# Two DMAs and a VectorE addition in place of a folding product between two MLP layers, with a new order of issue

## The chip, the cores and the metric

One core of one Trainium2 chip. The metric is the device time of one execution in microseconds (us); lower is better. A change within 0.2% cannot be told from none here.

## What is computed

Tokens are 2 x 4096 rows of 192 floats. A causal window of 7 rows is mixed with softmax weights per head, then two MLP layers follow, both 192 to 2048 to 192, in fp32:

```python
w = exp(weight_gen - max); w = w / (sum(w) + 1e-09)
x = einsum('bshk,bskhg->bshg', w, windows_of_7(x_pad))      # 8 heads, 24 columns each
h = x @ moe_w_in;   x = (h * sigmoid(h)) @ moe_w_out         # layer 1
h = x @ moe2_w_in                                            # layer 2
P = a[0] + a[1]*h + a[2]*h**2 + a[3]*h**3
Q = 1.0 + abs(b[0])*abs(h) + abs(b[1])*h**2
out = (P / (Q + 1e-06)) @ moe2_w_out
```

## The kernel before, in words

The 8192 tokens are worked in 16 blocks of 512, with the tokens along the free axis. The 192 columns are held as 128 rows and 64 more, the 64 stored twice in one 128-row half (`DL` is 64). Every operand of a product is split into a rounded high part and a low rest. The hidden 2048 rows are cut into 8 units of 256, so that a unit's intermediate is one PSUM tile of 128x1024 (the tag `h`, two buffers). The letters below are the names in the plan; a digit behind a letter is the unit.

- Attention of a block: loads `X` and `AW`, four rows of work `M`, `p`, `r`, `a` (VectorE or GpSimd, L436 to L455), a DMA `AD` that doubles the 64 columns, transposes `T` on TensorE, then `XH0` (ScalarE) and `XL0` (VectorE) split the result.
- Layer 1, unit u: product `A` (10 matmuls, L516), SiLU `S` in place (ScalarE, L553), its rounded part `H` (ScalarE, L557), the rest `L` (VectorE, L561), product `C` into the accumulator `acc0` (10 matmuls).
- Between the layers: the second half of `acc0` holds partial sums of the 64 columns on rows 0 to 63 and on rows 64 to 127. `EC` copies this half to SBUF, `EM` multiplies it with the matrix `fold` (two identities side by side, so that both row halves receive the sum) back into `acc0`; `XH1` and `XL1` split the result for layer 2.
- Layer 2, unit u: product `B`, then four readers of its PSUM tile: `U` (L592) and `V` (L596) on ScalarE, `u` (L602) and `w` (L605) on VectorE. The denominator goes `Y` (VectorE, L611), `N` (logarithm, ScalarE, L616), `G` (sigmoid, ScalarE, L619); `g` (VectorE, L622) makes the ratio, `h` and `l` split it, product `D` adds to `acc1`.
- The end of a block: `FC` copies `acc1` to the SBUF tile `of`, `FT` turns it back on TensorE, `FE` moves the result to the SBUF tile `o`, `O` stores it by DMA.
- Weights arrive as 64-bit floats and are decoded at the start, four VectorE operations for each piece, interleaved with blocks 0 and 1.

Nothing is scheduled at run time. A table of numbers (`KEYS`) gives each step a key; block b of the middle blocks adds 72 times b. All steps are sorted by key and issued in that order, each engine executing its own in order. A second table (`ENGINES`) picks one of the engines that a step may use. Blocks of a layer overlap: while block b is in layer 2, block b+1 is in layer 1 and the last units of layer 2 of block b-1 finish. Buffers are counted in `BUFS`; a step that takes a buffer waits for the last reader of its former content. Readers of one PSUM tile on different engines wait for one another in the order of issue. All DMAs leave from one queue, SyncE's.

Of the kernel before, what the change touches and what calls it, by code (L numbers as in the profile page):

```python
# [19 lines left out]
JB = 4  # L20
# [23 lines left out]
    q0B03:-316.92 q0A12:-309.71 q0B04:-303.11 s0n:-287.19 q0A2a:-276.83 q0B0d:-276.41 q0O11:-275.19 q0B0h:-271.54
    q0A13:-270.4 zM0:-265.19 q0O12:-257.47 q0A21:-246.3 q0A14:-238.64 zp0:-238.19 q0A22:-237.38 zr0:-229.4
    q0A23:-224.88 za0:-219.64 q0O13:-215.26 zM1:-214.13 q0A24:-200.03 q0O6l:-191.2 q0A3l:-175.29 q0A1h:-175.16
    q0A1x:-172.73 q0A3a:-168.08 zp1:-167.7 q0B1l:-164 q0A31:-160.72 q0O6a:-160.16 zr1:-157.97 q0O61:-156.06
    za1:-153.62 q0O62:-150.5 zM2:-148.24 q0O14:-147.91 zp2:-143.67 q0A32:-141.33 q0A2h:-139.04 zr2:-130.1
    q0B0x:-129.28 X:-122.84 za2:-121.15 q0O1h:-119.09 q0O63:-116.78 q0O3l:-114.33 zM3:-113.33 q0B1a:-108.33
    q0O1x:-107.5 zp3:-105.83 q0A33:-104.78 AW:-103.75 zr3:-103.7 M0:-102 q0B11:-99.99 p0:-99.17 q0O64:-98.62 r0:-95.49  # L50
    q0O3a:-95.08 za3:-94.88 q1A0l:-93.71 q0B12:-93.54 q0A34:-92.42 a0:-91.77 q0O31:-91.43 q0O6h:-90.26 M2:-89.49
    q0A2x:-89.37 q0B13:-87.76 zAD:-87.54 q0O32:-85.82 zT:-85.5 zXH0:-84.82 p2:-84.81 r2:-82.87 q0B14:-81.83 s1l:-79.62
    a2:-78.91 q0A3h:-77.37 s1m:-77.25 M1:-76.38 s1e:-75.48 zXL0:-74.15 q0O6x:-73.97 p1:-73.06 q0A3x:-72.06 r1:-70.26
    a1:-69.45 q1A0a:-68.21 q0O4l:-67.96 M3:-67.93 s1n:-67.64 q0O33:-67.46 q0O4a:-66.3 q0B1d:-63.09 q0B1h:-58.98
    p3:-58.27 q0O41:-58.11 r3:-57.41 a3:-56.23 zA0:-55.29 q1A01:-53.55 AD:-52.97 q1B0l:-52.39 q0O34:-52.26 s1s:-52.14
    q1B0a:-49.67 q0O42:-45.37 q1B1l:-41.31 q1A02:-40.81 q1B01:-38.11 zA1:-37.66 q1A03:-37.49 q1B02:-37.18 q0O3h:-36.98
    q1A04:-35.54 q0O3x:-35.3 zS1:-33.17 zS0:-32.69 T:-32.52 q1B03:-32.4 zH0:-31.67 q0O7l:-31.25 XH0:-30.06
    q1B04:-27.57 XL0:-26.97 zL0:-26.04 zA2:-25.83 q0O43:-25.64 zC0:-25.16 zH1:-25.08 A1:-23.94 q0O7a:-23.54
    q0B1x:-23.34 S1:-20.68 q1B0d:-19.55 q0O71:-19.39 zL1:-19.32 zS2:-19.15 cr:-18.63 zC1:-18.63 H1:-18.34 zA3:-18.22
    A0:-17.92 S0:-17.74 H0:-17.7 q0O44:-17.4 q0O5l:-17.27 L1:-17.17 L0:-15.84 q0O72:-14.6 zH2:-12.31 A2:-12.19  # L60
    C0:-11.95 S2:-11.05 zL2:-10.62 q0O5a:-10.18 H2:-9.74 q0O51:-9.49 q0O73:-8.85 zS3:-8.43 zH3:-8.32 L2:-7.53
    q1B0h:-6.59 q0O52:-6.44 zA4:-6.32 A3:-6.25 zL3:-4.99 zS4:-4.81 zC2:-3.95 C1:-3.35 q0O74:-3.01 q1B0x:-2.84 S3:-2.08
    q0O4h:-1.67 zA5:-0.78 q1B1a:0.17 zS5:0.67 H3:1.05 q0O53:1.19 L3:1.38 zH4:1.61 q1A3l:1.94 zC3:2.03 q0O4x:2.33
# [5 lines left out]
    L7:39.16 zL7:39.78 q1O0a:40.59 q1A1a:40.61 q1O01:41.22 q1A11:42.51 C7:42.68 zC6:44.87 q1A12:45.54 zC7:46.34
    zEC:47.04 EC:47.63 q1O02:47.96 EM:48.17 q1A13:48.18 q1B14:49.89 zEM:49.99 q1A33:50.18 q1A14:50.33 q1B1d:50.75  # L70
    XH1:50.98 q1A1h:52.25 zXH1:52.35 q1A1x:53.2 XL1:54.32 zXL1:54.44 zB2:55.99 B2:56.94 zU2:57.59 q1O03:57.63
    q1A34:58.12 q1O04:58.57 q1A3h:58.58 U2:59.61 V2:60.06 zu2:60.2 zV2:60.24 zw2:60.55 u2:60.8 q1O1l:60.82 q1A3x:60.89
    zY2:61.22 w2:61.87 zB0:62.37 B0:63.3 q1B1h:64.35 q1B1x:64.57 q1O1a:64.77 V0:65.24 q1O11:65.24 U0:65.35 Y2:66.19
# [653 lines left out]
```

## Time and profile before

| | |
|---|---|
| time, median of 3 runs | 1407.87 us (1406.32 to 1409.04) |
| time of the profiled execution | 1408.39 us |
| its span, first to last instruction | 1406.6 us |
| TensorE (PE) busy | 1247.3 us, 89% of the span, 5472 matmuls |
| VectorE (DVE) busy | 1144.8 us, 81% |
| ScalarE (ACT) busy | 1044.6 us, 74% |
| GpSimd (POOL) busy | 586.3 us, 42% |
| mean granted TensorE clock | 0.986 of full |

A busy share is the time in which an engine executes; the rest it waits, by its order, for another engine or a buffer. The rows further below come from views of one execution: the page, the table of busy time by stretch, the timeline of an engine, the chain of waits that ended last, and one line's durations.

### The profile page before, as it was taken

To read this page: it belongs to the slowest core of one execution; us is meant where nothing else is said; L and a number is where in the kernel's file an instruction comes from. 1 tells how busy PE (TensorE), PEld (TensorE's weight loads), DVE (VectorE), ACT (ScalarE), POOL (GpSimd) and SP (SyncE) were. 2 spreads that over 40 slices of the span, in tenths; PEclk is the share of its full clock that TensorE was granted. 3 is DMA by queue.
4 is the path that set the end of the run, shared out by engine and by line. 5 is a ranking of instruction groups with operands and counts; after the bars stand their busy time and mean duration, and the time that the engine had idled before them with its cause. 6 is when DMAs were issued, how large, how long until landed. Compare 5 with 4: busy or idle time off the path is not lost.

```text
span 1406.6 us, 14510 instructions
## 1 busy us (share of the span) xinstructions
PE 1247.3 (89%) x5472; PEld 1001.1 (71%) x5472; DVE 1144.8 (81%) x1073; ACT 1044.6 (74%) x1000; POOL 586.3 (42%) x328
## 2 busy tenths in 40 slices
...
DMA packets 24294, 45.00 MB, mean 32 GB/s; under 512 B 10404, under 2 KB 16674, under 8 KB 24224
## 3 DMA queue, kind: packets, MB, share of 16 engines
...
q8 instruction: 43, 0.70, 0.2%
...
## 4 chain that ended last, share of the span: by engine, by line
PE 63%; DVE 19%; issue 8%; ACT 7%; DMA 2%; SPq 0%; POOL 0%; DVEq 0%; ACTq 0%; POOLq 0%
PE h L516 33%; PE acc L540 5%; PE acc L537 5%; PE acc L538 5%; PE acc L539 5%; PE acc L541 5%; DVE t L602 5%; DVE t L605 4%; ACT y L596 3%; DVE g1l L561 2%; ACT t L592 2%; DVE y L611 1%; PE acc L577 1%; DMA aw<-wsm 1%; DVE pr L445 1%
## 5 line engine op out<-in xcount | busy, mean ns | idle before, releaser
L516 PE MATMUL h<-xh,wa 128*128 128x512 f32 x1024 | 329.6, 403 | 94.4 <-DVE g1l L561 55.3
L516 PEld LDWEIGHTS h<-xh,wa 128*128 128x128 f32 x1024 | 187.3, 191 | 159.9 <-issue 64.3
L217 POOL TENSOR_SCALAR g2h<-t 128x1024 fp32r<-128x1024 f32 x93 | 119.9, 1289 | 405.7 <-PE acc L539 388.6
L602 DVE TENSOR_TENSOR t<-t,h 128x1024 f32<-128x1024 f32 x128 | 155.4, 1215 | 101.0 <-ACT y L596 48.1
L632 POOL TENSOR_TENSOR g2l<-t,g2h 128x1024 fp32r<-128x1024 f32 x88 | 223.9, 2546 | 22.3 <-ACT g2h L215 14.5
L596 ACT ACTIVATE y<-h,b_sb 128x1024 f32<-128x1024 f32 x128 | 142.5, 1113 | 120.6 <-PE h L516 86.1
L611 DVE SCALAR_TENSOR_TENSOR y<-y,b_sb 128x1024 f32<-128x1024 f32 x128 | 205.2, 1615 | 25.0 <-ACT y L596 24.9
L592 ACT ACTIVATE t<-h,a_sb 128x1024 f32<-128x1024 f32 x128 | 153.9, 1203 | 68.6 <-PE h L516 67.6
L516 PE MATMUL h<-xl,wa 128*128 128x512 f32 x512 | 202.2, 395 | 2.3 <-DVE xl L493 2.3
L561 DVE TENSOR_TENSOR g1l<-h,g1h 128x1024 fp32r<-128x1024 f32 x128 | 156.0, 1219 | 57.4 <-ACT g1h L557 57.3
L516 PE MATMUL h<-xh,wb 128*128 128x512 f32 x512 | 202.3, 395 | 0.0
L516 PE MATMUL h<-xl,wb 128*128 128x512 f32 x512 | 201.5, 394 | 0.0
L622 DVE SCALAR_TENSOR_TENSOR t<-t,a_sb,y 128x1024 f32<-128x1024 f32 x128 | 188.1, 1489 | 2.6 <-ACT y L619 2.5
L436 POOL TENSOR_TENSOR pr<-xw,aw 128x1344 f32<-128x1344 f32 x45 | 139.2, 3093 | 117.9 <-DVE ao L455 117.9
L553 ACT ACTIVATE h<-h 128x1024 f32<-128x1024 f32 x128 | 129.0, 1008 | 62.5 <-PE h L516 59.0
L605 DVE SCALAR_TENSOR_TENSOR t<-t,a_sb,h 128x1024 f32<-128x1024 f32 x128 | 163.7, 1280 | 14.1 <-ACT y L596 9.8
L616 ACT ACTIVATE y<-y,c_sb 128x1024 f32<-128x1024 f32 x128 | 146.6, 1148 | 9.3 <-DVE y L611 8.9
L557 ACT ACTIVATE g1h<-h 128x1024 fp32r<-128x1024 f32 x128 | 130.8, 1023 | 16.7 <-PE acc L539 14.3
L619 ACT ACTIVATE y<-y 128x1024 f32<-128x1024 f32 x128 | 125.9, 1048 | 0.4
L516 PEld LDWEIGHTS h<-xl,wa 128*128 128x128 f32 x512 | 97.5, 190 | 24.7 <-DVE xl L493 3.4
L516 PEld LDWEIGHTS h<-xh,wb 128*128 128x128 f32 x512 | 97.7, 191 | 21.5
L516 PEld LDWEIGHTS h<-xl,wb 128*128 128x128 f32 x512 | 97.4, 190 | 21.3
...
## 6 DMA issues: line engine op xcount, KB each, us to landing
...
raw<-in_moe_w_out_dram SPq DMA_DIRECT2D x16, 384.0 KB, 3.2
out_dram<-o SPq DMA_DIRECT2D x16, 384.0 KB, 5.8
...
dup<-dec SPq DMA_DIRECT2D x16, 128.0 KB, 2.3
ao<-ao SPq DMA_DIRECT2D x16, 128.0 KB, 2.4
...
```

The costliest lines, as they stand in the source:

```text
L436: e.tensor_tensor(out=p.rearrange("p k (h g) -> p k h g", g=G), in0=st[xw][:, j:j + K, :].rearrange("p k (h g) -> p k h g", g=G), in1=weig ...
L516: pe.matmul(out=h[:, i], lhsT=w[:, f], rhs=xx, start=(n == 0), stop=(n == len(terms) - 1))
L557: act.activation(out=t, in_=st[hb], func=AF.Copy)
L561: dve.tensor_tensor(out=t, in0=st[hb], in1=st[gh].bitcast(F32), op=ALU.subtract)
L592: act.activation(out=q, in_=st[hb], func=AF.Identity, scale=a_sb[:, 3:4], bias=a_sb[:, 2:3])
L596: act.activation(out=q, in_=st[hb], func=AF.Abs, scale=b_sb[:, 1:2])
L602: dve.tensor_tensor(out=st[t], in0=st[t], in1=flat(), op=ALU.mult)
L605: dve.scalar_tensor_tensor(out=st[t], in0=st[t], scalar=a_sb[:, 1:2], in1=flat(), op0=ALU.add, op1=ALU.mult)
L611: dve.scalar_tensor_tensor(out=st[y], in0=st[y], scalar=b_sb[:, 0:1], in1=st[y], op0=ALU.add, op1=ALU.mult)
L616: act.activation(out=st[y], in_=st[y], func=AF.Ln, scale=c_sb[:, 0:1], bias=1e-6)
L622: dve.scalar_tensor_tensor(out=st[t], in0=st[t], scalar=a_sb[:, 0:1], in1=st[y], op0=ALU.add, op1=ALU.mult)
L632: e.tensor_tensor(out=q, in0=st[t], in1=st[gh].bitcast(F32), op=ALU.subtract)
```

## The change

The folding product `EM` goes. The tile `of` in the role of `e` now has two halves: `EC` copies into the first, two DMAs (`EM`, now on SyncE's queue) write the first's rows 64 to 127 into the second's rows 0 to 63 and the other way round, and a VectorE addition `EA` adds the second half to the accumulator in PSUM. The tile `o` is gone: `FE` writes its result over `of`, and `O` stores from there, so that the next `EC` must wait until that store has read it. The buffers of `y` go from 4 to 5. Block 1 gets keys of its own (prefix y), as blocks 0 (z) and 15 (e) had; all keys and the choice of engines are new.

```diff
-    zEC:47.04 EC:47.63 EM:48.17 q1A13:48.18 q1B14:49.89 zEM:49.99 q1A33:50.18 q1A14:50.33 q1B1d:50.75
+    yS3:47.283 q1O3x:47.615 EC:47.948 EM:48.099 yH3:48.169 zB3:48.825 zU3:49.187 yC1:51.102 q1O63:51.941 yL3:53.318
...
 BUFS = dict(
-    h=2, acc0=1, acc1=1, xw=1, aw=2, pr=1, ao=1, xh0=1, xl0=1, xh1=1, xl1=1, of=1, o=1,
-    g1h=2, g1l=2, y=4, t=5, g2h=2, g2l=2,
+    h=2, acc0=1, acc1=1, xw=1, aw=2, pr=1, ao=1, xh0=1, xl0=1, xh1=1, xl1=1, of=1,
+    g1h=2, g1l=2, y=5, t=5, g2h=2, g2l=2,
 )
...
         def copy(e):
-            st[ev] = t = new("of", [P, 2 * BT], name="e")[:, 0:BT]
-            round_to(e, t, st[acc][:, 1])
+            st[ev] = t = new("of", [P, 2 * BT], name="e")
+            round_to(e, t[:, 0:BT], st[acc][:, 1])
+
+        def swap(e):
+            t = st[ev]
+            for i in range(2):
+                sp.dma_start(out=t[i * DL:(i + 1) * DL, BT:], in_=t[(1 - i) * DL:(2 - i) * DL, 0:BT])
 
         def sums(e):
-            pe.matmul(out=st[acc][:, 1], lhsT=fold, rhs=st[ev], start=True, stop=True)
+            dve.tensor_tensor(out=st[acc][:, 1], in0=st[acc][:, 1], in1=st[ev][:, BT:], op=ALU.add)
...
-        plan.op("EM", b, "PE", sums, rd=[(*ev, 0), ("ident", 0)], wr=[(*acc, 0)])
+        plan.op("EM", b, "SP", swap, rd=[(*ev, 0)], wr=[(*ev, 0)])
+        plan.op("EA", b, "DVE", sums, rd=[(*acc, 0), (*ev, 0)], wr=[(*acc, 0)])
...
         def evac(e):
-            st[o] = t = new("o", [P, JB, D])
+            t = st[of].rearrange("p a c -> p (a c)")[:, 0:JB * D].rearrange("p (j d) -> p j d", d=D)
+            st["o", b] = t
             round_to(e, t, st[tp][:, :, 0:D])
```

All lines of the key table are replaced; the two shown are the ones with the steps between the layers. What the tables do is seen in the order in which the built programs issue.

ScalarE, a middle block, from a SiLU `S7` to the split `XH1` of the sums between the layers. Before: L553 is `S`, L557 `H`, L596 `V`, L592 `U`, L616 `N`, L619 `G`, L489 `XH`; a table load precedes a function of another kind.

```order
L553 ACTIVATE h<-h 128x1024
L616 ACT_TABLE_LOAD
L616 ACTIVATE y<-y,c_sb 128x1024
L557 ACTIVATE g1h<-h 128x1024
L596 ACTIVATE y<-h,b_sb 128x1024
L616 ACTIVATE y<-y,c_sb 128x1024
L592 ACTIVATE t<-h,a_sb 128x1024
L616 ACTIVATE y<-y,c_sb 128x1024
L489 ACTIVATE xh_4463<-tp 128x1024
L616 ACTIVATE y<-y,c_sb 128x1024
L619 ACT_TABLE_LOAD
L619 ACTIVATE y<-y 128x1024 x4
```

The same place in the changed kernel, from the logarithms `N4`, `N5` ahead of `S7`: L650 is `N`, L581 `S`, L653 `G`, L585 `H`, L243 here `FE`, L517 `XH`.

```order
L650 ACT_TABLE_LOAD
L650 ACTIVATE y<-y,c_sb 128x1024 x2
L581 ACT_TABLE_LOAD
L581 ACTIVATE h<-h 128x1024
L653 ACT_TABLE_LOAD
L653 ACTIVATE y<-y 128x1024
L585 ACTIVATE g1h<-h 128x1024
L243 ACTIVATE of<-to 128x768
L650 ACT_TABLE_LOAD
L650 ACTIVATE y<-y,c_sb 128x1024
L517 ACTIVATE xh_4470<-tp 128x1024
L653 ACT_TABLE_LOAD
```

Logarithms, SiLUs and sigmoids stood in runs of their kind; now they alternate, with a load at each turn. In the whole program the loads go from 114 to 214, in a middle block from 6 to 13. `FC` and `FE` of the middle blocks have come to ScalarE from VectorE.

VectorE at the turn between the layers, before: the copy `EC` is L219 `e<-acc`, `XL1` is L493 `xl_4553`.

```order
L493 TENSOR_TENSOR xl_4484<-tp,xh_4463 128x1024
L219 COPY e<-acc_4051 128x512
L219 COPY o<-to 128x768
L449 TENSOR_TENSOR pr<-pr 128x384
L622 SCALAR_TENSOR_TENSOR t<-t,a_sb,y 128x1024
L455 TENSOR_TENSOR ao<-pr 128x192
L622 SCALAR_TENSOR_TENSOR t<-t,a_sb,y 128x1024
L493 TENSOR_TENSOR xl_4553<-acc_4051,xh_4529 128x1024
```

The same place now: L610 is the addition `EA`, L636 `u`, L639 `w`, L589 `L`, L656 `g`, L521 `XL`.

```order
L521 TENSOR_TENSOR xl_5050<-tp,xh_5021 128x1024
L247 COPY e<-acc_4592 128x512
L656 SCALAR_TENSOR_TENSOR t<-t,a_sb,y 128x1024
L477 TENSOR_TENSOR pr<-pr 128x384
L483 TENSOR_TENSOR ao<-pr 128x192
L656 SCALAR_TENSOR_TENSOR t<-t,a_sb,y 128x1024
L610 TENSOR_TENSOR acc_4592<-acc_4592,e 128x512
L636 TENSOR_TENSOR t<-t,h 128x1024
L589 TENSOR_TENSOR g1l<-h,g1h 128x1024
L521 TENSOR_TENSOR xl_5122<-acc_4592,xh_5102 128x1024
L639 SCALAR_TENSOR_TENSOR t<-t,a_sb,h 128x1024
L473 TENSOR_TENSOR pr<-pr 128x576
```

Four VectorE instructions stand between the copy and the addition. Behind the addition, and so behind the two DMAs, come `u7`, `L0`, `XL1` and `w7`, the last being the last reader of a PSUM tile.

The TensorE order of a middle block in the changed kernel is, in the plan's names (+1 is the next block, -1 the one before): C7, B7-1, A0+1, D2-1, D3-1, A1+1, B2, C0+1, A2+1, C1+1, B0, A3+1, D4-1, B1, D5-1, B3, C2+1, A4+1, C3+1, B5, D6-1, A6+1, D7-1, A5+1, C4+1, B4, B6, D0, A7+1, D1, C5+1, FT-1, C6+1, T+2, and C7+1 again. ScalarE's, from `V1` of the block on (with / for a table load): V1 U1 / N2 N0 V3 U3 N1 N3 / S4 H4 / G1 V5 U5 G3 G0 G2 / S6 H6 S5 FC H5 h0 V4 U4 U6 V6 / N4 N5 / S7 / G4 H7 FE / N6 XH0 / G5 G6 V7 U7 / S0 H0 XH1. `M0` and `p1` have gone from VectorE to GpSimd; `l0`, `l2`, `l3`, `l5`, `r2` and `h1` from GpSimd to VectorE.

## Rows read from the trace of the kernel before

**Rows 1.** Busy time by stretch, cut where the 16 folding products start or blocks group

```profile
core 0: us, PE busy (x) PEld busy (x) DVE busy (x) ACT busy (x) POOL busy (x), PEclk, DMA share, GB/s
0.00:114.25 114.25, 47.61 (x187) 36.40 (x187) 86.48 (x151) 44.50 (x62) 24.73 (x24) 0.94 0.51 141
114.25:202.64 88.39, 70.02 (x281) 53.73 (x280) 72.05 (x86) 69.13 (x68) 29.51 (x27) 0.95 0.16 47
202.64:286.44 83.80, 76.16 (x333) 60.21 (x332) 72.77 (x66) 68.26 (x65) 35.36 (x22) 0.99 0.07 20
286.44:366.81 80.37, 76.70 (x343) 62.01 (x342) 65.75 (x57) 61.89 (x59) 37.31 (x19) 1.00 0.07 21
366.81:1251.98 885.17, 843.50 (x3764) 682.30 (x3763) 730.73 (x623) 688.20 (x645) 413.41 (x212) 1.00 0.07 22
1251.98:1328.33 76.35, 75.22 (x336) 61.43 (x335) 58.14 (x48) 60.35 (x57) 22.38 (x13) 1.00 0.03 11
1328.33:1406.60 78.27, 58.15 (x237) 45.02 (x235) 58.92 (x48) 52.31 (x47) 23.58 (x13) 0.91 0.03 11
```

**Rows 2.** The chain that ended last: start, length, a product's ten matmuls

```profile
650.98 2.27 PE h L516 x10
```

**Rows 3.** PE timeline of a middle block: start, length, instruction, idle before it

```profile
668.42 0.70 PE L516 MATMUL h<-xh,wa 128*128 128x512 f32 x2 [1.58 <-DVE g1l L561]
...
689.59 1.02 PE L577 MATMUL acc<-e,fold 128*128 128x512 f32 x2
...
690.68 0.40 PE L538 MATMUL acc<-g2h,wo 128*128 128x512 f32 x1
```

**Rows 4.** ACT timeline of a middle block, and two rows of the end

```profile
671.03 1.21 ACT L592 ACTIVATE t<-h,a_sb 128x1024 f32<-128x1024 f32 x1 [2.74 <-PE h L516]
672.13 1.10 ACT L596 ACTIVATE y<-h,b_sb 128x1024 f32<-128x1024 f32 x1
673.23 1.01 ACT L553 ACTIVATE h<-h 128x1024 f32<-128x1024 f32 x1
674.26 1.28 ACT L616 ACT_TABLE_LOAD   x1
675.55 1.15 ACT L616 ACTIVATE y<-y,c_sb 128x1024 f32<-128x1024 f32 x1
676.61 1.01 ACT L557 ACTIVATE g1h<-h 128x1024 fp32r<-128x1024 f32 x1
...
686.13 3.90 ACT L619 ACTIVATE y<-y 128x1024 f32<-128x1024 f32 x4
...
1399.46 1.02 ACT L215 ACTIVATE of<-acc 128x1024 f32<-128x1024 f32 x1 [11.15 <-PE acc L541]
1401.93 0.81 ACT L215 ACTIVATE o<-to 128x768 f32<-128x768 f32 x1 [1.45 <-PE to L660]
```

**Rows 5.** DVE timeline of a middle block

```profile
628.05 2.73 DVE L611 SCALAR_TENSOR_TENSOR y<-y,b_sb 128x1024 f32<-128x1024 f32 x1 [0.78 <-ACT y L596]
...
643.50 1.21 DVE L602 TENSOR_TENSOR t<-t,h 128x1024 f32<-128x1024 f32 x1
644.74 1.28 DVE L605 SCALAR_TENSOR_TENSOR t<-t,a_sb,h 128x1024 f32<-128x1024 f32 x1
...
687.42 0.69 DVE L219 COPY e<-acc 128x512 f32<-128x512 f32 x1 [1.78 <-PE to L660]
```

**Rows 6.** Durations of the denominator step on DVE, ns min/median/max

```profile
L611 DVE SCALAR_TENSOR_TENSOR y<-y,b_sb x128: 1272/1280/3581, 126.6 to 1382.5; 128x1024 f32<-128x1024 f32 x128
```

**Rows 7.** POOL timeline, the work beside the first row of Rows 5

```profile
626.15 3.54 POOL L436 TENSOR_TENSOR pr<-xw,aw 128x1344 f32<-128x1344 f32 x1 [2.88 <-DVE ao L455]
```

**Rows 8.** Issue durations on SyncE's queue of the weights' DMAs inside SBUF

```profile
L355 SPq DMA_DIRECT2D dup<-dec x16: 485/588/602, 21.3 to 116.7; - x16
```

**Rows 9.** Page, part 6: DMA issues with size and time to landing

```profile
out_dram<-o SPq DMA_DIRECT2D x16, 384.0 KB, 5.8
...
dup<-dec SPq DMA_DIRECT2D x16, 128.0 KB, 2.3
```

More of the change, by code (lines that the diff above doesn't have):

```diff
@@ L44 @@
[L44 to L63, printed above, removed]
@@ L69 @@
[L69 to L73, printed above, removed]
@@ new lines @@
+    q0O2h:-1739.82 q0B0d:-1736.66 q0A02:-1725.96 q0A1l:-1702.71 q0B0h:-1658.16 q0O03:-1644.78 q0O04:-1637.27
+    q0A03:-1622.71 q0O0h:-1589.04 q0O6a:-1548.27 q0A04:-1539.2 q0A3l:-1532.67 q0O2x:-1506.98 q0A0h:-1485.47
+    q0O61:-1471.06 q0O62:-1222.76 s0m:-1222.04 q0O63:-1184.06 q0O64:-1181.21 q0A0x:-1178.74 q0B1l:-1155.86
+    q0O3l:-1152.08 zX:-1141.9 q0O6h:-1137.28 q0O0x:-1127.08 q0O6x:-1123.86 q0A1a:-1119.13 q0O3a:-1106.14
+    q0A3a:-1087.37 q0A11:-1077.61 q0A31:-1051.29 q0O31:-1041.27 q0O1l:-1030.01 q0B0x:-1018.44 s0e:-1007.59
@@ new lines @@
+    q0B14:-680.047 zr1:-661.877 q0O52:-657.523 q0O1h:-656.302 za1:-656.264 q0O7l:-643.536 q0O3x:-640.257
+    q0B1d:-622.621 q0O43:-619.567 q0O7a:-614.523 zM2:-601.162 q0O44:-595.622 zp2:-581.528 q0O1x:-580.902
+    q1A0l:-578.764 zr2:-573.772 q0O71:-570.533 za2:-566.352 q0O72:-562.921 zM3:-562.816 q0B1h:-557.218 q0O53:-545.215
+    q1A3l:-534.125 zp3:-533.845 q0O54:-527.519 zr3:-519.993 q1A0a:-516.091 q0O5h:-510.966 q1A01:-506.491 za3:-504.439
+    q1B0l:-480.957 q0O73:-478.544 zAD:-476.922 q0O5x:-472.583 q0B1x:-471.86 q1B0a:-470.828 q1A2l:-467.485
@@ new lines @@
+    q1A02:-467.451 q1A3a:-464.232 q1B01:-463.057 q0O74:-460.995 cl:-457.201 s1l:-449.652 q1A03:-444.455 zT:-438.888
+    q0O4h:-432.152 q1B1l:-431.777 q1B02:-430.679 zXH0:-426.07 q1A04:-419.877 q0O7h:-417.605 q1B03:-415.963
+    zXL0:-391.078 q1A0h:-388.969 q0O7x:-385.52 q1A31:-381.818 q0A2l:-380.003 q1B04:-362.412 q1A0x:-349.852
+    zA2:-346.827 q1A32:-344.449 q1O2l:-343.433 q1B0d:-339.698 zA0:-337.735 q0O4x:-336.072 q0A2a:-330.552
+    q1A33:-329.541 q0A21:-325.537 q1B1a:-317.87 q1A34:-316.417 q1A2a:-315.724 q1B0h:-315.277 zS2:-307.372
@@ new lines @@
+    zC6:-33.947 zS7:-32.799 yAD:-30.313 T:-29.782 q1O51:-29.571 q1O52:-29.136 yT:-28.293 XH0:-26.983 XL0:-25.189
+    A0:-24.886 q1O12:-24.846 q1A14:-22.4 q1O4a:-21.076 q1O41:-20.047 zH7:-19.044 S0:-18.733 H0:-18.687 zL7:-17.117
+    L0:-16.779 A1:-15.897 q1O6l:-15.117 S1:-13.872 C0:-13.168 H1:-12.47 L1:-12.296 q1A1h:-8.498 A2:-6.923 yXH0:-6.641
+    S2:-6.536 H2:-5.788 zC7:-5.696 zEC:-5.633 C1:-5.039 q1O33:-3.823 L2:-2.948 cr:-1.944 yXL0:-0.426 A3:-0.007 S3:0.35
+    H3:1.313 q1A1x:1.586 yA1:1.888 q1O6a:1.91 L3:1.946 yS1:2.689 q1O13:4.85 q1O14:5.093 C2:6.875 q1O42:7.17
@@ new lines @@
+    L7:42.774 zY0:43.381 zu2:43.94 q1O3h:44.44 zN2:45.673 zN0:45.883 C7:45.885 yC0:46.799 yA3:46.945 zw2:47.019
+    yS3:47.283 q1O3x:47.615 EC:47.948 EM:48.099 yH3:48.169 zB3:48.825 zU3:49.187 yC1:51.102 q1O63:51.941 yL3:53.318
+    zu3:53.749 EA:54.235 XH1:54.351 yA2:54.507 zw3:54.782 XL1:56.913 B2:57.496 zG0:57.54 zV3:57.585 yS2:57.666
+    q1O64:57.815 q1O6h:58.861 q1O4x:59.365 U2:59.57 q1O6x:60.693 V2:61.139 yH2:61.559 zB1:62.745 zg0:63.608 u2:63.653
+    zU1:64.423 yL2:65.022 zB5:65.981 zV1:66.208 w2:66.507 zG2:66.54 Y2:67.07 zu1:67.732 B0:68.302 zw1:68.382
@@ new lines @@
+    yu1:150.977 yN1:151.717 zh7:152 yB3:152.39 g7:152.743 yw1:152.894 zD6:154.537 yU3:155.03 yG0:155.122 yu3:155.885
+    yw3:155.891 yG1:156.208 h7:158.943 yV3:159.4 zl7:160.219 yY3:161.623 yg0:161.669 yg1:162.043 yB5:162.122
+    l7:162.166 yU5:162.382 yV5:162.947 yu5:163.173 D6:163.446 yN2:164.595 yN3:164.734 yw5:164.989 zD7:165.53
+    zFC:166.691 yY5:167.282 D7:168.734 yh1:168.91 FC:170.661 yl1:170.797 yh0:171.073 yG3:171.502 yB4:172.882
+    yl0:174.058 yU4:174.367 yV4:175.271 yu4:175.939 yB6:176.798 yD0:177.025 yw4:177.036 yG2:178.098 yV6:179.415
@@ new lines @@
+    yU6:179.618 yN5:180.046 yY4:180.081 yu6:181.605 FT:181.739 yw6:182.304 yg3:182.973 zFT:183.016 FE:183.803
+    yY6:184.873 zFE:185.334 yG5:187.269 zO:187.325 yg2:188.96 yh2:189.422 yl2:190.172 yB7:190.459 yg5:190.605
+    O:190.719 yD1:191.927 yN6:192.014 yN4:193.259 yD2:195.969 yV7:196.038 yU7:196.225 yu7:196.815 yw7:198.48
+    yG4:198.983 yG6:199.468 yh5:200.852 yY7:201.255 yh3:202.837 yl3:203.522 yg4:204.883 yD3:205.583 yN7:205.98
+    yh4:206.425 yG7:206.712 yl4:211.366 yl5:211.474 yg6:211.897 yD4:214.567 yh6:215.662 yD5:219.757 yl6:220.865
@@ new lines @@
+    ew2:1146.51 eY2:1147.07 eB0:1148.3 eU0:1149.82 eV0:1149.87 eu0:1151.26 ew0:1152.7 eY0:1154.43 eB1:1154.86
+    eV1:1155.09 eU1:1156.94 eN2:1157.5 eY1:1157.9 eB3:1158.7 eu1:1159.07 eN0:1159.08 ew1:1159.53 eV3:1159.63
+    eY3:1162.68 eU3:1163.82 eu3:1166.2 eN1:1166.77 ew3:1167.67 eN3:1167.71 eG1:1169.84 eB5:1170.14 eg1:1170.99
+    eV5:1172.22 eh1:1172.46 eU5:1172.49 eu5:1173.61 ew5:1174.44 eG3:1174.64 eG0:1175.95 eg0:1176.09 eG2:1176.85
+    el1:1177.13 eY5:1178.35 eg3:1178.75 eB4:1179.61 eh0:1180.48 eV4:1181.12 el0:1181.52 eB6:1181.59 eY4:1182.8
```

139 lines of the change are left out of this document (76 added, 63 removed).

## The prediction, made before the changed kernel ran

> **What bounds the kernel now.** I read the busy time by stretch first [rows 1]. The folding products cut the run into a start (to 286.4 us, up to block 2's), a middle with a constant rhythm, and an end. From 366.81 to 1251.98 lie 11 periods, 885.17 / 11 = 80.47 us each (nine ordinary ones of about 80.4, as the row of 286.44, two that also prepare softmax weights). In the ordinary one TensorE works 76.70 of 80.37 us and idles 3.67; VectorE works 65.75 and ScalarE 61.89. So TensorE bounds the middle, by its own work; what it waits for is a PSUM tile that its last VectorE reader frees late, such as 1.58 us behind an `L` [rows 3]. Ten matmuls take 2.27 us [rows 2], and a period has 32 such groups.
>
> The profiled execution took 1408.39 us, 1.8 more than its span of 1406.6, and 0.5 more than the median of 1407.87. The sum below is made on the span; the device time adds 1.8.
>
> **The folding product.** It starts at 689.59, and the second matmul behind it at 690.68; less 0.23 for the matmul between, it holds TensorE 0.86 us [rows 3]. 16 times that is 13.8 us of TensorE's work. This is a gain only where TensorE stays the bound.
>
> **What takes its place.** Once the copy `EC` has ended, the first DMA is issued in about 0.6 us [rows 8], the second as long after, and one of this kind lands 2.3 us after its issue [rows 9]: both are in after 0.6 + 2.3 = 2.9 us. The addition is half as wide as a 1.21 us addition with a PSUM operand [rows 5]; the copy of the same 128x512 took 0.69, so I take 0.69 (bounds 0.6 and 0.8). The path from copy to split thus goes from 0.86 to 3.6 us. TensorE's cover is B7, A0, D2, D3 and A1 ahead of B2, five groups or 11.3 us. On VectorE g4, r0, a0 and g5 stand ahead of the addition, some 3.4 us at their undisturbed lengths, so the wait for the DMAs costs about nothing there. I cost the swap at nothing. Without its cover (`u7` waits behind the addition, and `L0`, `XL1`, `w7` behind that) each us beyond the slack comes back in full; by the walk below `L0` waits for `H0` until some 1.5 us after `u7` could be done, and that is the slack.
>
> The store: `EC` now waits until `O` has read `of`. A store landed in 5.8 us (median) [rows 9]. Before, it was issued right behind the 960 KB load of `X`; now `X` is issued far earlier in the period, so I expect some 3 us; `FE` ends about 4 us ahead of `EC`. Bounds: nothing, or 1.3 us of which the slack takes all. I take nothing.
>
> **ScalarE.** The order shows 13 table loads in a middle block for 6. A load takes 1.28 us, and the next instruction starts 1.29 after it [rows 4]: 7 x 1.29 = 9.0 us. `FC` 1.02 and `FE` 0.81 come from VectorE [rows 4]. ScalarE's busy time becomes 61.89 + 9.0 + 1.8 = 72.7 us a period, nearly as full as TensorE. The Trainium skill ("ScalarE: Activation LUTs", What ACT_TABLE_LOAD costs) states about 1283 ns for the load and about 1380 ns for a drain at every switch. The load agrees with the row, the drain does not: SiLU's successor load starts 1.03 us after the SiLU, and the logarithm 1.29 after the load [rows 4].
>
> So I walked one period by the new orders, from the end of `w7`, which frees the tile for A1+1, to the next `w7`. Three legs follow one another.
> 1. TensorE: A1, B2, C0, A2, C1, B0, A3, D4, B1, 9 x 2.27 = 20.4, and 0.5 for restarts and two short waits (A3 on `L2`, B1 on `w0`): **20.9**. B1's chain `U0 V0 u0 w0` takes 1.10 + 1.10 + 1.24 + 1.28 = 4.7 [rows 4, 5] beside the 4.5 of A3 and D4.
> 2. ScalarE: from `V1` it has work without a gap up to `XH1`. Spacings [rows 4]: six pairs of U and V at 2.15, 12.9; seven N at 1.06, 7.4; seven G at 3.90 / 4 = 0.98, 6.9; five pairs of S and H at 2.03, 10.2; FC, FE, XH0, XH1 and h0 4.9; ten loads at 1.29, 12.9. Together **55.2**. One wait falls in: `N3` needs `Y3`, which stands on VectorE behind `w1` and `g7`: I find it 0.5 late. **0.5**.
> 3. VectorE: `XL1` 1.2, `w7` 1.28, handovers 0.1: **2.6**.
>
> That is 20.9 + 55.2 + 0.5 + 2.6 = **79.2 us** against 80.4. TensorE then has 76.7 - 0.9 = 75.8 us of work in it and idles 3.4: the folding product's time is gained, a little of the old idle time too, and ScalarE is the new bound for two thirds of the period.
>
> What the walk leaves open is a collision. A denominator step on VectorE lasts 1.28 us at the median and 3.58 at most [rows 6]; beside a multiplication on GpSimd it took 2.73 [rows 5, 7]. Such a stretch ahead of `N3` counts in full. GpSimd's work falls (four `l` leave it, `M0` and `p1` come), but `h6`, `r3`, `a3` and `h7` run where `Y0`, `g7` and `Y3` do. Bounds for `N3`'s wait: 0 and 1.9, so the period is 78.7 to 80.6. I take 0.5, since most of those steps are short. VectorE's busy time goes up about 2.5 us a period (four `l`, `h1`, `r2`, `EA` come; `M0`, `p1`, `FC`, `FE` go) to 68; it isn't full.
>
> **Start and end.** Up to block 0's fold VectorE was busy 86.5 of 114.25 us, then 72.1 of 88.4, then 72.8 of 83.8 [rows 1]. By the order, up to block 0's copy it has 95 decoding steps where 76 stood, and from there to block 1's 15 where 26 stood: work of the second stretch moves into the first, which has 28 us of idle VectorE. The second took 88.4 - 80.4 = 8.0 more than a period, the third 3.4. I take 2 us lost in the first, 7 gained in the second, 1 in the third: **-6**, with bounds of -14 (all 11.4 of surplus and some of the idle time) and +8 (the extra decoding stands ahead of `L2`, for which the third product waits).
> The last whole period (76.35) follows the ScalarE list without `XH0` and some loads: **-1**. In the end (78.27) no layer 1 work covers the swap, whose path is 2.7 us longer: **+3**, bounds 0 and +6.
>
> **The sum.** Middle: 11 x (79.2 - 80.4) = -13, and by the same two longer periods as before. 1406.6 - 13 - 6 - 1 + 3 = 1389.6 of span, 1391.4 of device time; I say **1392**. The likeliest case alone spans 1380 to 1404.
>
> **Rivals.**
> - *The VectorE step wins on the other side* (slower). GpSimd collisions hold `N3`, and through a full ScalarE the whole loop. For it: ScalarE has no gap in which to catch up, and 2.73 us was seen. Against it: GpSimd does less. It decides from `N3`'s wait of 1.7 us on, where the period passes 80.4. With 80.6 to 81.5, and nothing won at the start: 1406.6 + 11 x 0.2 to 1.1 + 2 + 1.8, about 1412 to 1422. Chance 0.17.
> - *TensorE stays the bound.* Table loads hide in waits and steps overlap, so the period falls to 75.8 and some 1 us of idle time, 76.8: 11 x -3.6 = -40, about 1364. For it: loads that stand ahead of a waiting instruction often cost nothing. Against it: by the list ScalarE does not wait from `V1` on. Chance 0.12.
> - *Nothing to measure.* The period stays within 0.3 of 80.4 and the start's gain goes at the end: 1405 to 1411. Chance 0.09.
> - *The store or the swap comes late* by 2.5 us more than I have it, 1 us beyond the slack: 80.2 a period, 1402. Chance 0.06; it lies within the range.
> - *A drain behind every load.* As a mechanism: 1.38 us at each of the ten loads of leg 2, 93 us a period, 1540. No row has such a gap; chance 0.01. It is what the cited section of "ScalarE: Activation LUTs" in the Trainium skill would give.
>
> The forecast has 0.55. Faster by over 0.2% (about what a measurement tells from no change) is under 1405: 0.55, 0.12 and 0.04 of the late store, 0.71. Within: 0.09 and 0.01 of the late store, 0.10. Slower: 0.17, the drain's 0.01 and 0.01 of the late store, 0.19. The range leaves out the lower half of TensorE's case and the upper half of the slow one: 1364 to 1414.
>
> **What would show it.** In the changed profile: a period of 79.2 between the copies; ScalarE busy 72 to 73 us in it and 214 loads in all, each 1.28; TensorE without L577 and idle 3 to 4 us, its longest wait for `w` at A1; `EA` rarely waiting for a DMA; on the chain that ended last ScalarE's share well up. It is wrong if ScalarE shows gaps between `V1` and `XH1` (TensorE's case), if `N3` waits for `Y3` by 2 us (the slow one), or if the copy waits for the store.

## The result, and the profile after

| | before | after |
|---|---|---|
| median | 1407.49 us (1406.32 to 1409.04, 4 runs) | 1365.10 us (1363.28 to 1366.69, 4 runs) |
| ratio, 95% interval | | 0.9698 [0.9681, 0.9715] |
| profiled execution: time, span | 1408.39, 1406.6 us | 1363.28, 1361.5 us |

The change is 42.4 us (3.0%) faster. The forecast was 1392 in a range of 1364 to 1414. So the sign was right, the time lies 1 us inside the fast end of the range, and the gain was 2.7 times as large as forecast.

The busy time by stretch of the changed kernel, cut where `XH1` of blocks 0, 1, 2, 3, 14 and 15 starts (us; then busy time and instructions of each engine, granted clock, DMA share, GB/s):

```profile
0.00:124.00 124.00, 52.53 (x196) 40.22 (x196) 102.02 (x187) 53.80 (x74) 13.76 (x24) 0.94 0.52 149
124.00:194.89 70.89, 63.12 (x264) 49.23 (x264) 58.39 (x64) 64.84 (x61) 33.18 (x23) 0.98 0.12 38
194.89:274.55 79.66, 76.81 (x343) 61.51 (x342) 65.69 (x62) 75.14 (x70) 35.34 (x19) 1.00 0.08 25
274.55:355.61 81.06, 78.98 (x353) 63.60 (x352) 67.72 (x60) 75.67 (x72) 32.72 (x17) 1.00 0.08 24
355.61:1214.77 859.16, 842.92 (x3742) 675.73 (x3741) 735.75 (x659) 798.43 (x743) 328.26 (x163) 1.00 0.09 26
1214.77:1288.27 73.50, 72.26 (x319) 57.77 (x318) 58.74 (x49) 67.93 (x64) 9.15 (x7) 1.00 0.03 10
1288.27:1361.50 73.23, 56.57 (x234) 42.45 (x232) 58.78 (x48) 56.62 (x53) 16.05 (x11) 0.94 0.03 11
```

They answer to [rows 1], whose cuts at the folding product stand 1.1 us ahead of `XH1` of the same block from block 2 on; two of them, from ScalarE's timeline of before:

```profile
287.50 1.03 ACT L489 ACTIVATE xh<-acc 128x1024 fp32r<-128x1024 f32 x1 [0.64 <-PE acc L577]
...
1329.38 1.04 ACT L489 ACTIVATE xh<-acc 128x1024 fp32r<-128x1024 f32 x1 [1.59 <-PE acc L577]
```

| stretch, from `XH1` to `XH1` | before | after | found | forecast |
|---|---|---|---|---|
| start, to block 2 | 287.50 | 274.55 | -13.0 | -6 |
| block 2 to 3 | 80.37 | 81.06 | +0.7 | in no term |
| 11 periods, block 3 to 14 | 885.16 | 859.16 | -26.0 | -13 |
| block 14 to 15 | 76.35 | 73.50 | -2.9 | -1 |
| block 15 to the end | 77.22 | 73.23 | -4.0 | +3 |
| span | 1406.6 | 1361.5 | -45.1 | -17 |

(The rows depend on the cut, since the swap moves `XH1` against the copy. Cut at the copy `EC`, the start is -17.1, block 2 to 3 +0.6, the middle -26.1, block 14 to 15 0.0 and the end -2.5. Each column is one execution. In the runs below that leave the start alone, `XH1` of block 0 comes at 124.0 to 127.7 us, so the start is known to some 3 us.)

Of the middle periods nine ordinary ones take 77.78 us and the two with softmax work 79.6. One ordinary period, from `XH1` to `XH1`, in the same columns:

```profile
981.42:1059.19 77.77, 76.58 (x342) 61.44 (x341) 65.85 (x59) 72.16 (x68) 30.54 (x16) 1.00 0.08 25
```

TensorE now idles 1.2 us of it (before 3.67 of 80.37). Its busy time hardly fell, from 76.70 to 76.58, so the period is shorter almost wholly by waits that are gone, and not by work that is gone. ScalarE is busy 72.16 where 72.7 was forecast. The chain that ended last, before and after, by engine:

```profile
PE 63%; DVE 19%; issue 8%; ACT 7%; DMA 2%; SPq 0%; POOL 0%; DVEq 0%; ACTq 0%; POOLq 0%
```

```profile
ACT 50%; PE 27%; DVE 12%; issue 7%; DMA 2%; SPq 0%; POOLq 0%; POOL 0%; ACTq 0%; DVEq 0%
```

The chain went from TensorE to ScalarE. Pieces of ScalarE's timeline in a period after, from `V1` to `XH1` of the next block (they answer to [rows 4]; L630 is `V`, L626 `U`, L650 `N`, L581 `S`, L585 `H`):

```profile
1004.45 1.12 ACT L630 ACTIVATE y<-h,b_sb 128x1024 f32<-128x1024 f32 x1
1005.46 1.20 ACT L626 ACTIVATE t<-h,a_sb 128x1024 f32<-128x1024 f32 x1
1006.68 1.28 ACT L650 ACT_TABLE_LOAD   x1
1007.98 2.19 ACT L650 ACTIVATE y<-y,c_sb 128x1024 f32<-128x1024 f32 x2
...
1032.33 1.12 ACT L630 ACTIVATE y<-h,b_sb 128x1024 f32<-128x1024 f32 x1 [0.21 <-PE h L544]
...
1035.09 1.21 ACT L626 ACTIVATE t<-h,a_sb 128x1024 f32<-128x1024 f32 x1 [0.55 <-PE h L544]
...
1058.27 1.03 ACT L585 ACTIVATE g1h<-h 128x1024 fp32r<-128x1024 f32 x1
1059.19 1.02 ACT L517 ACTIVATE xh<-acc 128x1024 fp32r<-128x1024 f32 x1
```

In these 55.8 us the view names two waits, 0.21 and 0.55, both for TensorE's products: apart from them ScalarE has no gaps, as the second leg said. The 0.5 that the leg had at `N3` did not come. VectorE in the same period (they answer to [rows 5]; L247 is `EC`, L656 `g`, L610 `EA`, L636 `u`, L589 `L`, L521 `XL`, L639 `w`):

```profile
1051.67 0.68 DVE L247 COPY e<-acc 128x512 f32<-128x512 f32 x1
1052.27 1.28 DVE L656 SCALAR_TENSOR_TENSOR t<-t,a_sb,y 128x1024 f32<-128x1024 f32 x1
...
1054.32 1.28 DVE L656 SCALAR_TENSOR_TENSOR t<-t,a_sb,y 128x1024 f32<-128x1024 f32 x1
1055.52 0.69 DVE L610 TENSOR_TENSOR acc<-acc,e 128x512 f32<-128x512 f32 x1
1056.12 1.21 DVE L636 TENSOR_TENSOR t<-t,h 128x1024 f32<-128x1024 f32 x1
1059.33 1.23 DVE L589 TENSOR_TENSOR g1l<-h,g1h 128x1024 fp32r<-128x1024 f32 x1 [2.00 <-ACT g1h L585]
1060.47 1.22 DVE L521 TENSOR_TENSOR xl<-acc,xh 128x1024 fp32r<-128x1024 f32 x1
1061.60 1.27 DVE L639 SCALAR_TENSOR_TENSOR t<-t,a_sb,h 128x1024 f32<-128x1024 f32 x1
```

`EA` starts behind `g5` without waiting for the DMAs; in the whole run it waits for them four times, 0.6 us at most. VectorE then waits 2.00 us for `H0` (ScalarE's row of 1058.27) before `L0`. And TensorE at `A1`, its second row here, with `B2` as the third:

```profile
1059.77 0.39 PE L569 MATMUL acc<-g2l,wo 128*128 128x512 f32 x1
1060.61 0.73 PE L544 MATMUL h<-xh,wa 128*128 128x512 f32 x2 [0.45 <-DVE g1l L589]
...
1063.04 0.69 PE L544 MATMUL h<-xh,wa 128*128 128x512 f32 x2
```

`A1` starts 0.84 us behind the matmul ahead of it, where 0.23 is the spacing. It waits for `L0`, which ends at 1060.56; `w7` has not even begun. `w7` ends at 1062.87, and `B2`, which takes the other PSUM buffer, starts at 1063.04 without a wait.

The denominator step `Y` after (it answers to [rows 6]), and the DMAs of the page's part 6 (to [rows 9]):

```profile
L645 DVE SCALAR_TENSOR_TENSOR y<-y,b_sb x128: 1274/1280/2143, 132.3 to 1343.0; 128x1024 f32<-128x1024 f32 x128
```

```profile
out_dram<-of SPq DMA_DIRECT2D x16, 384.0 KB, 2.3
...
e<-e SPq DMA_DIRECT2D x32, 128.0 KB, 2.3
```

### The profile page after: what moved, and what is told of

Same layout as the page of the kernel before. It is cut to its first block, busy times and chain, and to the rows that moved or that the text cites. A ratio compares the mean times of both kernels' runs of the same rounds, so it can differ in the third digit from the quotient of the medians.

```text
span 1361.5 us, 14596 instructions
## 1 busy us (share of the span) xinstructions
PE 1243.2 (91%) x5440; PEld 990.5 (73%) x5440; DVE 1147.1 (84%) x1128; ACT 1192.4 (88%) x1129; POOL 468.5 (34%) x260
## 4 chain that ended last, share of the span: by engine, by line
ACT 50%; PE 27%; DVE 12%; issue 7%; DMA 2%; SPq 0%; POOLq 0%; POOL 0%; ACTq 0%; DVEq 0%
PE h L544 17%; ACT y L650 7%; ACT L581 6%; ACT t L626 6%; ACT h L581 6%; ACT y L653 6%; ACT g1h L585 5%; ACT y L630 5%; ACT L650 4%; DVE g1l L589 4%; ACT L653 3%; PE acc L569 2%; PE acc L565 2%; PE acc L568 2%; PE acc L566 2%
## 5 line engine op out<-in xcount | busy, mean ns | idle before, releaser
L589 DVE TENSOR_TENSOR g1l<-h,g1h 128x1024 fp32r<-128x1024 f32 x128 | 156.5, 1224 | 117.1 <-ACT g1h L585 115.9
L464 POOL TENSOR_TENSOR pr<-xw,aw 128x1344 f32<-128x1344 f32 x56 | 176.2, 3146 | 208.5 <-DVE ao L483 205.2
L245 POOL TENSOR_SCALAR g2h<-t 128x1024 fp32r<-128x1024 f32 x77 | 94.0, 1221 | 353.7 <-PE acc L567 254.8
L656 DVE SCALAR_TENSOR_TENSOR t<-t,a_sb,y 128x1024 f32<-128x1024 f32 x128 | 166.1, 1301 | 18.7 <-ACT y L653 18.7
L626 ACT ACTIVATE t<-h,a_sb 128x1024 f32<-128x1024 f32 x128 | 153.7, 1201 | 27.2 <-PE h L544 26.2
L581 ACT ACTIVATE h<-h 128x1024 f32<-128x1024 f32 x128 | 129.2, 1010 | 52.0 <-PE h L544 41.9
L645 DVE SCALAR_TENSOR_TENSOR y<-y,b_sb 128x1024 f32<-128x1024 f32 x128 | 168.2, 1314 | 7.6 <-ACT y L630 4.8
L639 DVE SCALAR_TENSOR_TENSOR t<-t,a_sb,h 128x1024 f32<-128x1024 f32 x128 | 163.7, 1279 | 2.9
L636 DVE TENSOR_TENSOR t<-t,h 128x1024 f32<-128x1024 f32 x128 | 155.6, 1216 | 11.0 <-ACT y L630 5.2
L630 ACT ACTIVATE y<-h,b_sb 128x1024 f32<-128x1024 f32 x128 | 141.7, 1107 | 8.5 <-PE h L544 7.0
L650 ACT ACTIVATE y<-y,c_sb 128x1024 f32<-128x1024 f32 x128 | 142.5, 1148 | 2.8 <-DVE y L645 1.8
L666 DVE TENSOR_TENSOR g2l<-t,g2h 128x1024 fp32r<-128x1024 f32 x92 | 139.8, 1522 | 2.6 <-POOL g2h L245 2.5
L585 ACT ACTIVATE g1h<-h 128x1024 fp32r<-128x1024 f32 x128 | 131.1, 1025 | 4.7 <-PE acc L567 1.3
L666 POOL TENSOR_TENSOR g2l<-t,g2h 128x1024 fp32r<-128x1024 f32 x36 | 89.5, 2487 | 131.5 <-DVE g2h L247 130.2
L653 ACT ACTIVATE y<-y 128x1024 f32<-128x1024 f32 x128 | 130.4, 1056 | 0.7
```

The costliest lines, as they stand in the source:

```text
L464: e.tensor_tensor(out=p.rearrange("p k (h g) -> p k h g", g=G), in0=st[xw][:, j:j + K, :].rearrange("p k (h g) -> p k h g", g=G), in1=weig ...
L581: act.activation(out=st[hb], in_=st[hb], func=AF.Silu)
L585: act.activation(out=t, in_=st[hb], func=AF.Copy)
L589: dve.tensor_tensor(out=t, in0=st[hb], in1=st[gh].bitcast(F32), op=ALU.subtract)
L626: act.activation(out=q, in_=st[hb], func=AF.Identity, scale=a_sb[:, 3:4], bias=a_sb[:, 2:3])
L630: act.activation(out=q, in_=st[hb], func=AF.Abs, scale=b_sb[:, 1:2])
```

## The experiments

All times are medians of four runs (five for the last), with the kernel before at 1407.3 to 1407.6 beside them. Theory A in the expectations is the one formed from the two traces: the order of issue makes the gain, through a loop `H0`, `L0`, `A1` that runs over both ScalarE and TensorE.

**1. The folding product back, in the new order.**

```diff
-        plan.op("EM", b, "SP", swap, rd=[(*ev, 0)], wr=[(*ev, 0)])
-        plan.op("EA", b, "DVE", sums, rd=[(*acc, 0), (*ev, 0)], wr=[(*acc, 0)])
+        plan.op("EM", b, "PE", sums, rd=[(*ev, 0), ("ident", 0)], wr=[(*acc, 0)])
```

> The changed kernel with the folding product back on TensorE in the place of the two DMAs and the addition, all keys and engines as in the change. Theory A (the new order made the gain, the swap little): the product comes between A0 and D2, ahead of A1, which waits only 0.4 us there; a period gets 0.4 to 0.9 us longer, 12 periods 5 to 10 us, so 1370 to 1376. Theory B (the swap made most of the gain): the time goes back most of the way, 1395 or more.

Measured: 1364.31 us (1363.85 to 1364.70), ratio 0.9690 [0.9676, 0.9705]. The period is 77.8 to 77.9, and the block's end is as short as with the swap (73.6 from block 14 to 15). TensorE's timeline there:

```profile
977.94 1.02 PE L605 MATMUL acc<-e,fold 128*128 128x512 f32 x2
...
983.12 0.39 PE L569 MATMUL acc<-g2l,wo 128*128 128x512 f32 x1
983.35 0.61 PE L544 MATMUL h<-xh,wa 128*128 128x512 f32 x2
```

The product runs two groups (`D2`, `D3`) ahead of `A1`, and now `A1` follows at 0.23 us, with no wait: the product's 0.86 us stand where the changed kernel waits 0.61. All of the gain thus lies in what this run keeps: the keys, the choice of engines, the fifth buffer of `y` and the missing tile `o`. These were not taken apart. By the key table five `y` are in use at `V3` of each middle block, so the order as it stands uses the fifth buffer. The swap gives nothing on top. Even the 1370 to 1376 of theory A gave it too much.

**2. The swap alone, in the old order.** The kernel before with the two DMAs and `EA`, and a key for it:

```diff
+    EA:50.9 zEA:52.3 eEA:1129.5
```

> The kernel before with the two DMAs and the addition in place of the folding product, its own keys kept; the addition stands just ahead of the split XH1. Theory A: TensorE bounds the old order, its 0.86 us a block go, 13 us at most, and some of it comes back where XH1 is late: 1394 to 1405. Theory B: most of the 42 us are had, under 1380.

Measured: 1425.60 us (1424.02 to 1428.09), ratio 1.0127 [1.0108, 1.0147], slower than all that was expected. From `XH1` of block 3 to that of block 14 the middle takes 895.1 us for 885.2. Who waits, in us, times and longest one:

```profile
ACT xh L489 <- DVE acc L582: 26.4, 14, 2.0
...
DVE e L219 <- PE to L666: 23.2, 13, 1.9
```

In the kernel before, `XH1` waited for the folding product:

```profile
ACT xh L489 <- PE acc L577: 12.5, 15, 2.9
```

`XH1` waits for `EA` by up to 2.0 us in 14 blocks: in the old order, with this key for `EA`, the swap's path is not covered. The ordinary periods are some 0.5 us longer (80.8 to 81.1). About half of the middle's loss is in one period, block 13 to 14 (83.6 for 78.9), in which TensorE's granted clock was at half for 6.8 us. The other wait, of the copy behind the old block's end, was there before too ([rows 5], 1.78).

**3. One table load less.** In the changed kernel the sigmoid `G4` moves beside `G5`: 201 loads for 214.

```diff
-    G4:110.481
+    G4:118.3
```

> The changed kernel with one sigmoid of the middle blocks (G4) moved beside G5 and G6, which saves one ScalarE table load a period (201 for 214). Theory A, the loop runs through a full ScalarE: 1.28 us less a period up to what TensorE has idle there (1.2 us): 4 to 14 us faster, 1351 to 1361. Theory C, TensorE's own work is the bound again: no change, 1363 to 1367.

Measured: 1369.26 us (1366.89 to 1370.29), ratio 0.9723 [0.9706, 0.9741]: a load of 1.28 us less in each block, and 0.35 us more in each period (78.13). This is slower than both theories had it. ScalarE's timeline shows why:

```profile
1049.63 1.02 ACT L585 ACTIVATE g1h<-h 128x1024 fp32r<-128x1024 f32 x1 [0.93 <-PE acc L567]
1051.16 0.81 ACT L243 ACTIVATE of<-to 128x768 f32<-128x768 f32 x1 [0.51 <-PE to L694]
```

`H7` now waits 0.93 us for TensorE and `FE` 0.51. The time that the load took away becomes a wait, and `G4` lengthens the list behind it. So ScalarE's list up to `H7` does not alone set the period.

**4. `L0` behind `XL1`**, and `A1` behind it, so that `L0` ends later and `w7` keeps its place. It asks which of the two frees the tile of `A1`.

```diff
-    L0:-16.779 A1:-15.897
+    L0:-15.05 A1:-15.0
```

> The changed kernel with the step L0 of the middle blocks behind XL1 on VectorE (and A1 behind it in the order of issue), so that the PSUM tile for A1 comes free later. Theory A, the loop closes through H0, L0 and A1: XL1 waits for XH1, so L0 ends 2.1 us later and a period takes about 2 us more, 20 to 27 us in all, 1385 to 1392. Theory D, as I had predicted, the tile of A1 comes from w7, which stays where it was: no change within 3 us.

Measured: 1398.05 us (1397.30 to 1400.61), ratio 0.9935 [0.9915, 0.9955]. Block 3 to block 14 takes 891.5 us, 32.3 more than in the changed kernel: the whole loss lies in the middle. TensorE at `A1`, then VectorE:

```profile
1010.33 0.73 PE L544 MATMUL h<-xh,wa 128*128 128x512 f32 x2 [2.50 <-DVE g1l L589]
```

```profile
1007.92 1.23 DVE L521 TENSOR_TENSOR xl<-acc,xh 128x1024 fp32r<-128x1024 f32 x1 [2.91 <-ACT xh L517]
1009.06 1.22 DVE L589 TENSOR_TENSOR g1l<-h,g1h 128x1024 fp32r<-128x1024 f32 x1
```

`A1` starts as `L0` ends (1010.28), with `w7` behind it at 1010.20 to 1011.47. What frees the tile for `A1` is `L0`; theory D, the tile of my prediction, falls. But the loss is above the 20 to 27 us of theory A. `A1` waits 2.50 us for 0.45, 2.05 more. The five periods of the eleven in which TensorE's granted clock stayed at full (2.4 GHz) are 1.9 to 2.0 us longer than in the changed kernel (the ordinary ones 79.7 to 79.8): there the delay passes into the period nearly in full. In the other six the granted clock fell to half (1.2 GHz) as `A1` began (from 0.6 us before that to 1.5 after), for 3.4 us, in one period 6.8. These periods take 81.3, the one 82.7. In the columns of [rows 1], a stretch at the low clock behind the `A1` of 929.01, and the same place in a period without it, behind the `A1` of 849.25:

```profile
930.23:933.64 3.41, 3.41 (x9) 2.67 (x9) 2.70 (x4) 0.97 (x1) 1.76 (x1) 0.50 0.00 0
850.23:853.64 3.41, 3.41 (x16) 2.78 (x16) 2.94 (x5) 1.72 (x2) 1.52 (x1) 1.00 0.01 2
```

Nine matmuls are done where else sixteen are; seven at 0.23 us are 1.6 us, which is 81.3 less 79.7. So of the middle's 32 us some 22 are the wait behind `L0`, and some 11 the clock.

**5. Block 1 by the common keys** instead of its own:

```diff
-        own_key = "" if name[0] in "qsc" else {0: "z", 1: "y", NB - 1: "e"}.get(b, "")
+        own_key = "" if name[0] in "qsc" else {0: "z", NB - 1: "e"}.get(b, "")
```

> The changed kernel with block 1 issued by the common keys (its own, prefix y, unused). Up to block 2's copy the change gained 15.7 us. Theory S (block 1's own order made the start's gain): block 2's copy comes 8 to 16 us later than in the change, 1373 to 1381, with the same periods of 77.8 from there. Theory W (the order of the weights and of block 0 made it): within 3 us of the change, 1362 to 1368.

Measured: 1398.07 us (1396.17 to 1399.53), ratio 0.9931 [0.9916, 0.9946], a loss of 33 us, all ahead of block 3, for 8 to 16 expected; the periods behind are 77.8 again. Two of the waits between 120 and 235 us:

```profile
PE h L544 <- ACT xh L517: 17.5, 1, 17.5
...
ACT dec L353 <- POOL wa L410: 10.2, 1, 10.2
```

The common keys put block 1's work behind the weights' decoding. It shows that this table needs block 1's own order, but not how the start's 13 us divide between that order and the new order of the decoding: the edit makes a collision that neither kernel has. TensorE's granted clock is also lower in these 115 us, 0.84 of full on average for 0.99 in the changed kernel, and its share of the loss is not told apart.

**6. The swap twice**, four DMAs where two stand:

```diff
-            for i in range(2):
+            for i in (0, 1, 0, 1):
```

> The changed kernel with the two DMAs between the layers issued a second time behind the first (same data), so that the addition comes some 2.3 us later. Theory A (slack: VectorE idles 2.0 us behind u7 for H0 in the change): the addition takes up that idle time and a period grows by 0.2 to 0.5 us, in all 3 to 9 us with the end, 1367 to 1374. Theory F (the swap has no slack): 2.3 us a block, 16 times, about 1400.

Measured: 1373.48 us (1372.73 to 1374.63), ratio 0.9758 [0.9743, 0.9772]. In the middle, VectorE's timeline, and TensorE at the same `A1`:

```profile
989.40 0.70 DVE L610 TENSOR_TENSOR acc<-acc,e 128x512 f32<-128x512 f32 x1 [1.98 <-DMA e<-e]
990.01 1.21 DVE L636 TENSOR_TENSOR t<-t,h 128x1024 f32<-128x1024 f32 x1
991.15 1.23 DVE L589 TENSOR_TENSOR g1l<-h,g1h 128x1024 fp32r<-128x1024 f32 x1
```

```profile
992.43 0.73 PE L544 MATMUL h<-xh,wa 128*128 128x512 f32 x2 [0.45 <-DVE g1l L589]
```

`EA` now waits 1.98 us, `L0` follows `u7` without its 2.00, and `A1` waits 0.45 as in the changed kernel: a swap 2 us longer takes the slack and no more, and seven of the nine ordinary periods are 77.8 (two 78.4 and 78.6). So the time is within theory A's range, but not by longer periods. Most of the loss lies elsewhere: `XH1` of block 2 is 7.8 us later, and block 14 to 15 takes 2.0 us more.

**7 and 8. ScalarE's list shorter.** `FE` goes to VectorE; in the eighth run `FC` too.

```diff
-    FE:183.803
+    FE:186.4
-    EC:1 a0:1 a1:1
+    EC:1 FE:1 a0:1 a1:1
```

> The changed kernel with the step FE of the middle blocks on VectorE, where it idles ahead of L7, in place of ScalarE. Theory A (ScalarE's list between H7 and H0 lies in the loop): ScalarE loses 0.8 us there, 0.5 to 0.8 us a period, 12 periods, 1355 to 1360. Theory C (TensorE bounds each stretch, as when G4 was moved): within 2 us of the change.

Measured: 1360.36 us (1359.36 to 1363.07), ratio 0.9667 [0.9652, 0.9682]. The period is 77.51, 0.27 less, about half of the least that was expected.

```diff
-    FC:170.661
+    FC:171.5
-    EC:1 FE:1 a0:1 a1:1
+    EC:1 FE:1 FC:1 a0:1 a1:1
```

> As the run with FE on VectorE, and FC of the middle blocks too, behind L6 where VectorE waits for H5. Theory A: H5 and so L5 can come 0.26 us earlier (VectorE's copy ends then), 0.7 to 1.0 us a period in all, 1352 to 1358. Theory C: within 2 us of the change.

Measured: 1364.89 us (1362.95 to 1365.50), ratio 0.9692 [0.9675, 0.9708]. The ordinary period stays at 77.5, and the two with softmax work grow to 80.25 and 80.85: no further gain, and run 7's 4.7 us are lost again.

**9. The folding product and `FE` on VectorE together**, edits 1 and 7.

> The kernel with the folding product in the new order, and in it the copy FE on VectorE. Theory A (the order of issue makes the whole gain, the folding product stands in TensorE's wait ahead of A1, and FE on VectorE takes something from ScalarE's list behind H7): both effects add, period 77.4 to 77.7, time 1358 to 1362 us. Theory T (TensorE with the product in it is full at about 77.1 us of work per period, so that ScalarE's shorter list gives nothing): period 77.8, time 1363 to 1366 us.

Measured: 1364.85 us (1363.54 to 1366.10), ratio 0.9692 [0.9678, 0.9705]. The table by stretch of one period shows TensorE busy 77.05 of 77.80:

```profile
983.30:1061.10 77.80, 77.05 (x344) 61.98 (x343) 66.24 (x59) 71.78 (x68) 30.61 (x16) 1.00 0.06 21
```

With the product in it, TensorE's own list fills the period: the view names one wait in it, 0.40 us, and none at `A1`. A shorter ScalarE list gives nothing (theory T). Four runs now make a square:

| | `FE` on ScalarE | `FE` on VectorE |
|---|---|---|
| folding product | 77.85 a period, 1364.31 us | 77.80, 1364.85 |
| swap and addition | 77.77, 1365.10 (the change) | 77.51, 1360.36 |

Neither edit alone gives anything against the first cell; both together give 0.3 us a period and 4.0 us. By the periods of the other three cells the two limits, TensorE's list with the product and the loop through ScalarE, stand within 0.1 us of each other. The version with both edits beats the change by 4.7 us, with no run of the one inside the other's range; the intervals of the two ratios just touch.

## Why the prediction was right in its sign and wrong in its size

**Right.** ScalarE's busy time (72.16 for 72.7, 13 loads a middle block and 214 in all), the second leg (55.8 us for 55.7), `EA`'s 0.69, the swap hidden on VectorE (2.00 us of slack for 1.5, both DMAs in by about 3 us after the copy for 2.9), the store that costs nothing (2.3 us for "some 3"), ScalarE's share of the chain (from 7% to 50%). The collisions of `Y` with GpSimd, the slow rival, did not come: the longest `Y` fell from 3.58 to 2.14 us. Too high was only VectorE's busy time, 65.85 us a period for 68.

**Wrong, first step: the third leg.** It said "VectorE: `XL1` 1.2, `w7` 1.28, handovers 0.1", for a period that runs to "the end of `w7`, which frees the tile for A1+1". That tile is freed by `L0`; the one that `w7` frees goes to `B2`, and comes 0.17 us early. In the period shown, `A1` goes from 982.83 to 1060.61:
- first leg, to `V1` at 1004.45: 21.6 for 20.9;
- second leg, from there only to the end of `H0` at 1059.30: 54.9 for 55.7, as `XH1` no longer lies in the loop;
- third leg, from there through `L0` to `A1`: 1.3 for 2.6.

That is 77.8 for 79.2, or 1.4 us x 11 = 15 us; the middle's miss is 13. Run 4 ended `L0` some 2 us later and left `w7` in its place, and the periods went to 79.7, or 81.3 with the low clock. I had looked up the reader of the other one of the two PSUM buffers.

**Wrong, second step: "the folding product's time is gained".** Run 1 has the product and the whole gain. TensorE was to have 75.8 us of work in the period and to idle 3.4; it was busy for 76.58 and idled 1.2. The product fills a wait that the loop through ScalarE leaves on TensorE. Only with that loop shorter (runs 7 and 9) is the product worth something: 0.3 us of its 0.86 a period. The rule in the prediction's paragraph on the product, that this "is a gain only where TensorE stays the bound", was right and I did not apply it to my own result, in which ScalarE was the bound.

**Wrong, third step: the start.** "7 gained in the second" stretch: it was 18 (from `XH1` of block 0 to that of block 1, 89.1 to 70.9 us), against 8.6 lost in the first for 2 and 3.4 gained in the third for 1. So -13.0 for -6, near the bound of -14, and beyond it by the copies (-17.1). I took the surplus over a period as about the most that the stretch could give, but it became 7 us shorter than a middle period. Block 1's own order, which the old table had not, may be the reason; run 5 does not decide it.

**Wrong, fourth step: the end.** It had "no layer 1 work covers the swap, whose path is 2.7 us longer", +3. It came out at -4.0 (by the copies -2.5), and with the product in its place (run 1) the end is 0.8 us longer, not shorter. What in the last block's order makes the end shorter was not tried.

**The rival that had the time.** The rival "TensorE stays the bound", at "about 1364", named the time almost to the microsecond, and it is what put the time inside the range. That was luck. It had a period of 76.8, so -40 in the middle, which with the forecast's -4 for all the rest gives 1364. Found were 77.78, -26 and, for all the rest, -19. Its table loads were to hide in waits and gaps between `V1` and `XH1`, and ScalarE has no such gaps but the 0.8 us named above. Yet run 3 shows a part of it true: one load less bought only waits. TensorE is within 1.5% of full and ScalarE within 7.5%, and the loop goes over both; "which one is the bound" was the wrong question here.

In the Trainium skill, "ScalarE: Activation LUTs" (What ACT_TABLE_LOAD costs) gives about 1283 ns for the load and about 1380 ns for a drain. The row of 1006.68 agrees with the first, and shows no drain: the `U` ahead of it had ended 0.02 us earlier, and the logarithm starts 1.30 behind the load's start.

Still open: which of the many moves in the new order took away TensorE's waits in the middle, how the start's 13 us divide, and what shortens the end.
